# A chunked delta-rule attention with a feed-forward behind it: all work as tasks in an own order, with another mapping on TensorE

## The chip, the core and the metric

The kernel runs on one core of one Trainium2 chip. The metric is the device time of one execution in microseconds (us). Names of engines: PE is TensorE (PEld its weight loads), DVE is VectorE, ACT is ScalarE, POOL is GpSimd, SP is SyncE, which issues the transfers. L615 is line 615 of the kernel before; behind the change the line numbers are those of the new file.

## What is computed

Four batches of eight heads (32 in all), 768 steps, head size 40. Each head carries a 40 x 40 state; the rows of all heads then pass a layer norm and a feed-forward layer 320 -> 1280 -> 320.

```python
for t in range(S):
    kt, vt, rt = (k[:, :, t], v[:, :, t], r[:, :, t])
    wt, at, bt = (w[:, :, t], a[:, :, t], b[:, :, t])
    y[:, :, t] = np.einsum('bhd,bhde->bhe', rt, state)
    Sa = np.einsum('bhde,bhe->bhd', state, at)
    state_decay = state * wt[:, :, None, :] - np.einsum('bhd,bhe->bhde', Sa, bt)
    state = state_decay + np.einsum('bhd,bhe->bhde', vt, kt)
...
xn = (x - mu) / np.sqrt(var + 1e-06) * g_ln
ch = np.maximum(xn @ w_ch1, 0.0) @ w_ch2
return (x + ch).astype(np.float32)
```

## The kernel before

**Chunks.** The 768 steps are cut into 24 chunks of 32. Within a chunk the recurrence is turned into matrix products and one unit-triangular 32 x 32 system per head; from chunk to chunk only the state is carried. The 32 heads lie in two halves of 16, one at partitions 0 to 39 (or 0 to 31), one at 64 to 103.

**Preparation** (`prep`, L140 to L195): `wa` (decays and a) and `bk` (b and k) are loaded with the channel on partitions. Two scans (`gE` L149, `qE` L153) give the running products of the decays from both ends, `aT` (L160) and `bk` (L165) are scaled by them, on DVE for the first six chunks and on POOL behind them. ACT copies `aT` into a block-diagonal tile `abd` (L164), so that one matmul with 104 rows serves both halves (L178). The signed triangle `gk` (L183) goes to DRAM (`d_g`).

**Token rows** (`load_cl`, L309 to L345): the same decays, keys and b are loaded a second time with the token on partitions (`clt`), checked for values outside the range that the chunk form allows (`wild`, L315), scanned again (`gC` L321, `qC` L325), transposed on DVE (L329, L331) and multiplied on POOL into `xk` in eight small pieces a chunk (L339).

**Triangles.** Chunks are gathered into slabs of two or four, so that one system stands on each partition (64 or 128 of them). `invert2` (the first three slabs) inverts both 16 x 16 diagonal halves in 14 steps of two DVE instructions (L241, L245), and `solve2` joins them by three rounds of matmuls; `invert` (the other five slabs) inverts the whole 32 x 32 in 30 steps (L208, L211). The result goes to DRAM and comes back as `tt`.

**Chain** (`chain`, L366 to L393): the right-hand side (`prh`, L372), times the inverse (L357 in `solve`, L268 in `solve2`), copied into `x2` (L362, L279), the new state (L384), scaled into the next chunk's `x2` (L390). **Rows out** (`state` L401, `post` L416 to L447): transposes, the masked product with r (L429, L435), the output rows (L443), `xt` (L447). **Feed-forward** (`norm` L557 to L589, `moe` L593 to L637), called MoE in the code: two chunks make a group of 256 rows; for each of ten slices of 128 hidden units, eight matmuls (L615), a relu and its remainder (L618, L619), and six matmuls of the slice before (L601). Weights are converted from 64-bit floats at the start (L488 to L531).

**Order.** DVE and ACT run the first stage in the written order; behind it priorities (`BOOST`, `NUDGE`) and a scheduler's timeline decide. 180 matmuls on a constant (`warm`, L221) fill PE in the first 200 us. All transfers are issued by SP in one queue.

```python
def invert(si):
    ...
    for j in range(1, C - 1):
        ...
        nc.vector.tensor_tensor(
            out=tv, in0=y[0:n, j + 1:, j:j + 1].broadcast_to([n, m, j]),
            in1=y[0:n, j:j + 1, 0:j].broadcast_to([n, m, j]), op=ALU.mult)
        final["inv", si] = nc.vector.tensor_tensor(
            out=y[0:n, j + 1:, 0:j], in0=y[0:n, j + 1:, 0:j], in1=tv, op=ALU.add)
...
for q in range(4):
    hf, p = q % 2, 8 * (q // 2) + h
    nc.tensor.matmul(
        prh[32 * q:32 * q + 32, h], lhsT=X2s[RROW[hf], hf, 32 * p:32 * p + 32],
        rhs=X2[RROW[hf], hf, p, 0:D], start=True, stop=True)
```

## Time and profile before

| | before |
|---|---|
| median of 3 runs | 703.12 us (701.27 to 704.05) |
| the profiled execution | 704.42 us |
| its span, first to last instruction | 702.6 us |
| mean granted TensorE clock | 0.898 |
| moved by DMA | 92.35 MB, 158156 packets |

A row of a view of lines reads: line, engine, operation, output<-inputs, shapes and count, then busy time and the mean of one in ns, then the idle time of the engine just before these instructions and what ended most of it. A row of the timeline reads: start in us, length in us, engine, line, operation. A matmul in fp32 leaves two records, one in fp32r or a transpose one. Matmuls are pipelined, so two rows may overlap; what a batch costs is seen from the start of one to the start of the next.

### The profile page before, as it was taken

To read this page: it belongs to the slowest core of one execution; us is meant where nothing else is said; L and a number is where in the kernel's file an instruction comes from. 1 tells how busy PE (TensorE), PEld (TensorE's weight loads), DVE (VectorE), ACT (ScalarE), POOL (GpSimd) and SP (SyncE) were. 2 spreads that over 40 slices of the span, in tenths; PEclk is the share of its full clock that TensorE was granted. 3 is DMA by queue.
4 is the path that set the end of the run, shared out by engine and by line. 5 is a ranking of instruction groups with operands and counts; after the bars stand their busy time and mean duration, and the time that the engine had idled before them with its cause. 6 is when DMAs were issued, how large, how long until landed. Compare 5 with 4: busy or idle time off the path is not lost.

```text
span 702.6 us, 24730 instructions
## 1 busy us (share of the span) xinstructions
PE 579.0 (82%) x10386; PEld 511.0 (73%) x10386; DVE 564.0 (80%) x1291; ACT 328.7 (47%) x816; POOL 291.4 (41%) x328
## 2 busy tenths in 40 slices
PE   2787778786697879788878889798987899999994
PEld 2686666675586758776757778697776777889994
DVE  8969899899589967899957999788996999764621
ACT  4314664544243445363366356444656255666220
POOL 8606486757514246146505533543133312233000
PEclk9979796868588799899989899999999899999998
DMA  6787977538635467455558653775336435420100
GB/s 176 202 230 206 280 188 182 136 86 198 137 104 144 99 154 161 124 159 134 131 145 177 141 134 94 169 167 122 89 95 116 117 86 119 109 51 16 38 20 22
DMA packets 158156, 92.35 MB, mean 131 GB/s; under 512 B 126504, under 2 KB 136488, under 8 KB 158040
## 3 DMA queue, kind: packets, MB, share of 16 engines
q1 hardware_dynamic: 158040, 90.72, 52.2%
q8 instruction: 83, 1.36, 0.8%
q14 instruction: 33, 0.27, 0.1%
HBM read 72.06 MB, written 18.64 MB: 129 GB/s over the span
## 4 chain that ended last, share of the span: by engine, by line
DVE 45%; PE 26%; DMA 17%; issue 5%; ACT 3%; SPq 2%; POOL 1%; DVEq 0%; POOLq 0%; ACTq 0%
PE ps L615 8%; PE ps L601 7%; DVE yinv L211 6%; DVE ytmp L208 6%; DMA yinv<-d_g 6%; DMA wa<-in_et_dram 4%; DVE x L390 3%; DVE x5s L435 3%; DVE gE L149 3%; DVE qE L153 3%; DVE hl L619 2%; DMA tt<-d_tt 2%; DVE yinv L245 2%; DMA d_tt<-yinv 2%; DVE gC L321 2%
## 5 line engine op out<-in xcount | busy, mean ns | idle before, releaser
L615 PE MATMUL ps<-xh,w 128*128 128x256 f32 x480 | 117.4, 303 | 3.3 <-DVE xl L589 2.3
L601 PE MATMUL ps<-w,hh 128*128 128x320 f32 x480 | 113.4, 330 | 4.9 <-DVE yinv L211 3.6
L618 ACT ACTIVATE hh<-ps 128x256 fp32r<-128x256 f32 x120 | 45.6, 383 | 140.0 <-PE ps L615 130.9
L615 PEld LDWEIGHTS ps<-xh,w 128*128 128x128 f32 x480 | 87.2, 200 | 8.4 <-DVE xl L589 2.6
L601 PEld LDWEIGHTS ps<-w,hh 128*128 128x128 f32 x480 | 79.2, 197 | 8.9 <-ACT hh L618 5.7
L601 PE MATMUL ps<-w,hl 128*128 128x320 f32 x240 | 75.0, 335 | 12.5 <-DVE hl L619 11.9
L619 DVE SCALAR_TENSOR_TENSOR hl<-ps,hh 128x256 fp32r<-128x256 f32 x120 | 49.5, 414 | 43.2 <-ACT hh L618 40.7
L208 DVE TENSOR_TENSOR ytmp<-yinv 128x30 f32<-128x30 f32 (+19 forms) x150 | 61.7, 412 | 26.4 <-DMA yinv<-d_g 24.4
L165 POOL TENSOR_TENSOR bk<-bk,gE 104x1024 f32<-104x1024 f32 x18 | 41.9, 2327 | 91.7 <-DMA bk<-in_et_dram 71.2
L221 PE MATMUL ps<-start,ident 128*128 128x160 f32 x360 | 74.3, 363 | 0.0
L615 PE MATMUL ps<-xl,w 128*128 128x256 f32 x240 | 71.0, 296 | 0.0
L221 PEld LDWEIGHTS ps<-start,ident 128*128 128x128 f32 x360 | 63.4, 232 | 2.3
L211 DVE TENSOR_TENSOR yinv<-yinv,ytmp 128x30 f32<-128x30 f32 (+19 forms) x150 | 61.1, 408 | 2.3
L601 PEld LDWEIGHTS ps<-w,hl 128*128 128x128 f32 x240 | 45.7, 199 | 16.5 <-DVE hl L619 14.9
L615 PEld LDWEIGHTS ps<-xl,w 128*128 128x128 f32 x240 | 48.2, 201 | 0.5
L362 ACT COPY x<-ps_c 32x160 f32<-32x160 f32 x144 | 40.7, 283 | 12.9 <-PE ps_c L357 9.7
L160 POOL TENSOR_TENSOR aT<-wa,qE 104x512 f32<-104x512 f32 x18 | 25.6, 1423 | 50.8 <-DVE qE L153 41.0
L390 DVE TENSOR_TENSOR x<-ps_c,x2s 40x320 f32<-40x320 f32 x92 | 44.7, 486 | 2.1
L384 PE MATMUL ps_c<-x,xk 128*40 128x40 f32 (+1 forms) x1472 | 43.1, 213 | 3.9 <-ACT x L279 2.9
L164 ACT COPY abd<-aT 40x512 f32<-40x512 f32 x48 | 29.6, 616 | 35.4 <-DVE aT L160 19.6
L372 PE MATMUL ps_c<-x,x2s 96*32 96x40 f32 (+1 forms) x1536 | 30.5, 223 | 18.7 <-issue 6.6
L384 PEld LDWEIGHTS ps_c<-x,xk 128*40 128x40 f32 (+1 forms) x1472 | 37.0, 126 | 9.2 <-ACT x L279 3.5
(174 smaller groups left out, 1359.7 us busy)
## 6 DMA issues: line engine op xcount, KB each, us to landing
clt<-in_cl_dram SPq DMA_DIRECT2D x24, 485.5 KB
wa<-in_et_dram SPq DMA_DIRECT2D x20, 422.9 KB
bk<-in_et_dram SPq DMA_DIRECT2D x20, 416.0 KB
d_g<-gk SPq DMA_DIRECT2D x48, 128.0 KB
x<-in_vt_dram SPq DMA_DIRECT2D x48, 128.0 KB
d_a<-aT SPq DMA_DIRECT2D x24, 214.5 KB
vu<-in_vr_dram SPq DMA_DIRECT2D x24, 208.0 KB
x2s<-d_a SPq DMA_DIRECT2D x48, 82.5 KB
```

What stands on the lines that cost most here:

```text
L165: (nc.gpsimd if c >= EARLY else nc.vector).tensor_tensor(out=kb, in0=kb, in1=g[R, :, 0:C].unsqueeze(2).broadcast_to([104, 16, 2, C]), op=A ...
L208: nc.vector.tensor_tensor(out=tv, in0=y[0:n, j + 1:, j:j + 1].broadcast_to([n, m, j]), in1=y[0:n, j:j + 1, 0:j].broadcast_to([n, m, j]), o ...
L211: final["inv", si] = nc.vector.tensor_tensor(out=y[0:n, j + 1:, 0:j], in0=y[0:n, j + 1:, 0:j], in1=tv, op=ALU.add)
L221: nc.tensor.matmul(pw[:, 0:w], lhsT=ident, rhs=start0.rearrange("p h t -> p (h t)")[:, 0:w], start=True, stop=True)
L362: nc.scalar.copy(out=dst[:, :, :, j, 0:D], in_=pu[32 * j:32 * j + 32, :, :, hf])
L372: nc.tensor.matmul(prh[32 * q:32 * q + 32, h], lhsT=X2s[RROW[hf], hf, 32 * p:32 * p + 32], rhs=X2[RROW[hf], hf, p, 0:D], start=True, stop= ...
L384: nc.tensor.matmul(pst[r0:r0 + D, h], lhsT=XK[FROW[hf], 1, hf, p], rhs=X2[FROW[hf], hf, p, 0:D], start=True, stop=True)
L390: nc.vector.tensor_tensor(out=X2n[r0:r0 + D, hf, ps, 0:D], in0=pst[r0:r0 + D], in1=pc.unsqueeze(2).broadcast_to([D, 8, D]), op=ALU.mult)
L601: nc.tensor.matmul(po[u], lhsT=l[:, us], rhs=ws[f"w2_{f}"][:, x], start=f == 0 and n == 0, stop=f == 9 and n == 2)
L615: nc.tensor.matmul(ph, lhsT=l, rhs=r, start=n == 0, stop=n == 7)
L618: nc.scalar.activation(out=hh, in_=ph, func=AF.Relu)
L619: nc.vector.scalar_tensor_tensor(out=hl, in0=ph, scalar=0.0, in1=hh.bitcast(F32), op0=ALU.max, op1=ALU.subtract)
```

## The change

A new kernel for the same inputs and outputs. No engine is left to the scheduler any more. Every piece of work is a task with an engine, an assumed duration, a key, and the names that it reads and writes; `Plan.order` plays the tasks through once while the kernel is built and writes the instructions down in that order. PSUM is eight banks, four for the small batches (A), two for the first feed-forward layer and the norm (H), two for the second layer (M).

```diff
+class Plan:
+    HOP = 0.15
+    def add(self, eng, us, fn, key, rd=(), wr=(), opens=(), late=0.0, kb=0.0, room=()):
...
+    def order(self, free):
...
+            if t["eng"] == "SP" and len(dma) >= 8:
+                s = max(s, dma[-8])
...
+                s0 = min(ss)[0]
+                s, n = min(((s, n) for s, n in ss if s <= s0 + 0.05), key=lambda x: T[x[1]]["key"])
...
+    with tc.manual_schedule():
+        for t in P.order(dict(A=[0, 1, 2, 3], H=[4, 5], M=[6, 7])):
+            t["fn"]()
```

**Token rows by TensorE.** The second load, its scans, transposes and small POOL products (`load_cl`) are gone. `prep` turns the scaled `bk` and the products `q` by matmuls with the identity into `kt` (L355, L360, copied by ACT at L364). A transfer and an ACT copy (L437) bring them into `xk`. The check of the decays reads them again in their first layout (`wilds`), 24 loads of 80 x 528 through the two `wa` buffers.

```diff
-        nc.vector.tensor_tensor_scan(
-            out=flat(g), data0=t[:, 0:330], data1=flat(start0[:, 0:10]), initial=0.0,
-            op0=ALU.mult, op1=ALU.max)
...
-        nc.vector.transpose(out=gt.rearrange("p (g j) -> p j g", j=10), in_=g[:, :, 0:C])
...
+                    if x < 2:
+                        for hf, rs in enumerate(ROWS):
+                            p = 8 * x + h
+                            mm(px[ZROW[hf]:ZROW[hf] + 64, h], lhsT=tb[rs, 64 * p:64 * p + 64],
+                               rhs=ident[rs, rs], start=True, stop=True)
+                    else:
+                        for y in range(4):
+                            rs = ROWS[y // 2]
+                            mm(px[32 * y:32 * y + 32, h], lhsT=q[rs, 8 * (y % 2) + h, 1:33],
+                               rhs=ident[rs, rs], start=True, stop=True)
```

**Triangles by halves.** All slabs hold two chunks (12 slabs, 64 partitions). `invert` loads three 16 x 16 quarters (`yv`), inverts the two diagonal ones in 14 steps (L387, L391); `merge` builds the missing quarter and the transposed inverse `tt` by two batches of 32-row quadrants (L411, L421).

```diff
+        dma(k0, 64, DL, [("y", i, 0)], yr(2), d_l[s][0:B, :, 0:B].rearrange("a m t -> m a t"))
...
+        for j in range(1, B - 1):
...
+            for h in range(8):
+                for qs in QUADS:
+                    mm(po[qs, h], lhsT=hv[i][qs, h, 0:2 * B], rhs=hv[i][qs, h, 2 * B:3 * B], start=True, stop=True)
...
+                    mm(po[qs, h], lhsT=qm[i][qs, h], rhs=hv[i][qs, h, 3 * B:5 * B], start=True, stop=True)
```

**Quadrants instead of block diagonals.** `abd`, `rbd` and `hbd` are gone. The triangle (L328) and the masked product (L532) use 40-row operands at partitions 0 and 64 in turn, the solution and its transpose (L463, L503) 32-row quadrants; the state is transposed by a matmul with the identity (L519). Evictions of L532 are two of 64 x 512 (L537) instead of four of 64 x 256.

```diff
-                nc.tensor.matmul(
-                    pz[64 * bb:64 * bb + 64, :, h], lhsT=vu[R, p].rearrange("p x t -> p (x t)"),
-                    rhs=rbd[R, p], start=True, stop=True)
...
+            for p in range(16):
+                for hf, rs in enumerate(ROWS):
+                    mm(pz[ZROW[hf]:ZROW[hf] + 64, p], lhsT=vu[i][rs, p].rearrange("p x t -> p (x t)"),
+                       rhs=x5s[i][rs, hf, p], start=True, stop=True)
...
+                    mm(bank[bs[bb].at][UROW[hf]:UROW[hf] + C, h * D:h * D + D], lhsT=tt[i][qs, h], rhs=hn[i][qs, h],
+                       start=True, stop=True)
```

The feed-forward's matmuls are the same (L714, L698), `warm` is gone, the output tile `ot` has two buffers instead of one, and the fourth chunk (not the sixth) is the last that scales on DVE (`EARLY`).

**Where it moves on the engines.** On PE, in the middle of the program, one chunk's small batches before (L429 and L178 the products with block diagonals, L384 the state):

```order
L601 MATMUL ps_4413<-w_5_2423,hl 128x320
L586 MATMUL ps_4888<-ident,xn 128x128 x2
L429 MATMUL ps_a<-rbd,vu 64x2x32 x2
L178 MATMUL ps_a<-abd,bk_93 64x2x32 x16
L429 MATMUL ps_a<-rbd,vu 64x2x32 x14
L586 MATMUL ps_4888<-ident,xn 128x128
L384 MATMUL ps_c<-x_1_96,xk_102 40x40 x32
```

And now at such a place (L421 the join of the triangles, L355 and L360 the token rows, L482 the state, L698 the feed-forward between them):

```order
L421 MATMUL bank_144<-hv_88,qm_90 32x32 x32
L355 MATMUL bank_145<-ident,bk_75 64x40 x16
L698 MATMUL bank_148<-w_8_1987,hh_135 128x320 x2
L698 MATMUL bank_148<-w_8_1987,hl_137 128x320
L698 MATMUL bank_149<-w_8_1987,hh_135 128x320 x2
L698 MATMUL bank_149<-w_8_1987,hl_138 128x320
L360 MATMUL bank_142<-ident,qE_79 32x40 x32
L482 MATMUL bank_143<-x_0_93,xk_99 40x40 x16
```

Sixteen matmuls over 104 rows became 32 over 40 rows, and four kinds of batches came in that PE did not have. On DVE, an inversion before, where the steps of one 32 x 32 system stand between other work (L390 the state, L149 to L153 the scans of a later chunk, L315 and L321 token rows):

```order
L208 TENSOR_TENSOR ytmp<-yinv 128x30
L390 TENSOR_TENSOR x_0_95<-ps_c,x2s_97 40x8x40 x2
L211 TENSOR_TENSOR yinv<-yinv,ytmp 128x30
L390 TENSOR_TENSOR x_0_95<-ps_c,x2s_97 40x8x40 x2
L208 TENSOR_TENSOR ytmp<-yinv 128x58
L149 SCALAR_TENSOR_TENSOR gE<-wa_91,start_88 104x528
L315 SCALAR_TENSOR_TENSOR wild<-clt,wild 128x320
L321 SCALAR_TENSOR_TENSOR gC<-clt,start_88 128x330
L211 TENSOR_TENSOR yinv<-yinv,ytmp 128x29x2
```

And now, slab 1 (`yv_85`), from the fill that waits for the slab's three loads:

```order
L379 MEMSET yv_85 64x16 x2
L387 TENSOR_TENSOR ytmp_86<-yv_85 64x28
L391 TENSOR_TENSOR yv_85<-yv_85,ytmp_86 64x2x14
L387 TENSOR_TENSOR ytmp_86<-yv_85 64x52
L391 TENSOR_TENSOR yv_85<-yv_85,ytmp_86 64x2x13x2
L387 TENSOR_TENSOR ytmp_86<-yv_85 64x72
L391 TENSOR_TENSOR yv_85<-yv_85,ytmp_86 64x2x12x3
```

The steps stand in a longer run behind the loads, with little between. On SP, the first transfers before and now (`wa`, `bk` the first chunks' inputs; `gt`, `rx`, `r_` weights; `vu` rows of v):

```order
L135 DMA wa_91<-in_et_dram 40x1041
L137 DMA wa_91<-in_et_dram 24x1041
L135 DMA wa_91<-in_et_dram 40x1041
L135 DMA bk_93<-in_et_dram 40x1024
L137 DMA bk_93<-in_et_dram 24x1024
L135 DMA bk_93<-in_et_dram 40x1024
```

```order
L227 DMA gt<-in_gl_dram 128x3
L227 DMA rx<-in_w1x_dram 128x640
L227 DMA r_0_0_223<-in_w_dram 128x256
L227 DMA r_1_0_224<-in_w_dram 128x256
L227 DMA r_0_225<-in_w_dram 128x320
L227 DMA r_1_226<-in_w_dram 128x320
L227 DMA vu_101<-in_vr_dram 40x16x32 x2
L227 DMA wa_73<-in_ea_dram 40x1041 x2
```

The first chunk's inputs now stand behind eight other transfers.

More of the change, by code (lines that the diff above doesn't have):

```diff
@@ L22 @@
 C = 32
+B = C // 2
 D = 40
@@ L474, in words @@
+    ws, raw, W1X = {}, {}, []
+    def weights():
+        dma(-2.0, 2, (), ["gt"], gt, gl)
+        op("ACT", 0.25, -1.8, (), ["gt"], lambda: nc.scalar.mul(out=gt, in_=gt, mul=2.0 ** -8))
+        raw["x"] = const.tile([128, FF], F32, name="rx", tag="w1x")
+        dma(-1.5, 655, (), [("w", "x")], raw["x"].bitcast(U64), w1x_in)
         def words(i):
@@ L762, in moes @@
-    def moes():
-        for g in range(NCH // 2):
-            while normed[0] < 2 * g + 2:
-                if normed[0] in xts:
-                    norm(normed[0])
-                    normed[0] += 1
-                yield
-            yield from moe(g, [out[2 * g], out[2 * g + 1]], g + 1 < NCH // 2)
-    def preps(first):
-        for c in range(first, NCH):
-            for i, _ in enumerate(p[c]):
-                if i < 2 and c + 2 < NCH:
-                    load_e(c + 2, [i])
-                yield
@@ L855, in body @@
     nc.vector.memset(ones, 1.0)
-    pf = ps_c.tile([1, 1], F32, name="ps_c")
-    nc.tensor.matmul(pf, lhsT=any_w, rhs=ones, start=True, stop=True)
+    fbank = [pf_.tile([128, 512], F32, name=f"fb{i}") for i in range(5)]
+    pf = fbank[0][0:1, 0:1]
+    mm(pf, lhsT=any_w, rhs=ones, start=True, stop=True)
     flag = const.tile([1, 1], mybir.dt.int32, name="flag")
```

1284 lines of the change are left out of this document (586 added, 698 removed).

## The prediction

> **What bounds the kernel now.** I read the totals first, then the same span in stretches.
>
> ```profile
> span 702.6 us, 24730 instructions
> PE 579.0 (82%) x10386; PEld 511.0 (73%) x10386; DVE 564.0 (80%) x1291; ACT 328.7 (47%) x816; POOL 291.4 (41%) x328
> DVE 45%; PE 26%; DMA 17%; issue 5%; ACT 3%; SPq 2%; POOL 1%; DVEq 0%; POOLq 0%; ACTq 0%
> ```
>
> The first row is the span, the second the busy time of each engine, the third the chain of waits that ended last. No engine is full: VectorE leads the chain, TensorE is as busy. The stretches show how the two share the time (their columns: length, PE, PEld, DVE, ACT, POOL busy, then granted TensorE clock, DMA share, GB/s).
>
> ```profile
> 0.00:35.00 35.00, 17.87 (x160) 16.75 (x160) 31.36 (x46) 14.10 (x18) 27.20 (x43) 0.98 0.70 189
> 50.00:100.00 50.00, 37.66 (x796) 32.91 (x794) 45.52 (x90) 25.29 (x59) 30.22 (x27) 0.86 0.85 232
> 100.00:150.00 50.00, 36.95 (x745) 31.42 (x747) 45.71 (x92) 25.67 (x63) 30.88 (x32) 0.76 0.60 149
> 250.00:350.00 100.00, 83.88 (x1564) 72.78 (x1563) 85.16 (x196) 48.49 (x126) 46.14 (x48) 0.91 0.60 148
> 350.00:450.00 100.00, 83.83 (x1516) 73.08 (x1515) 83.90 (x203) 49.79 (x131) 39.62 (x42) 0.91 0.59 139
> 450.00:550.00 100.00, 87.87 (x1617) 76.03 (x1617) 81.05 (x212) 55.67 (x145) 33.97 (x48) 0.95 0.53 125
> 550.00:650.00 100.00, 94.75 (x1770) 83.06 (x1768) 76.67 (x197) 56.04 (x148) 31.47 (x45) 1.00 0.34 78
> ```
>
> Two readings. In each 100 us from 250 to 650, PE and DVE busy add up to 168 to 171 us: when one has more to do the other gets less done, because chunk work and feed-forward work (MoE in the code) hand over between them. I call this sum **1.69** and use it as the coupling of two engines that work in fixed orders. And PE reached 0.95 once DVE needed only 0.77. Up to 150 us DVE is the full one (31.36 of 35, 45.5 of 50), and the feed-forward begins late:
>
> ```profile
> L615 PE MATMUL ps<-xh,w x480: 276/281/582, 136.0 to 691.5; 128*128 128x256 f32 x160
> ```
>
> **The change, engine by engine.** Everything is reissued, so I sum work, not edits.
>
> *TensorE.* Its price is the time from the start of one batch to the start of the next.
>
> ```profile
> 676.39 1.88 PE ps L615 x16
> 678.27 0.88 PE ps L601 x6
> 634.84 0.28 PE L615 MATMUL ps<-xl,w1x 128*128 128x256 f32 x1
> 635.05 0.80 PE L372 MATMUL ps_c<-x,x2s 96*32 96x40 f32 x64
> 635.78 0.83 PE L401 MATMUL ps_a<-ident,x 40*104 40x40 f32 x16
> 636.55 0.56 PE L601 MATMUL ps<-w,hh 128*128 128x320 f32 x2
> 636.94 0.31 PE L601 MATMUL ps<-w,hl 128*128 128x320 f32 x1
> 313.33 1.43 PE L384 MATMUL ps_c<-x,xk 128*40 128x40 f32 x64
> 314.68 0.38 PE L615 MATMUL ps<-xh,w 128*128 128x256 f32 x1
> 95.13 0.79 PE L268 MATMUL ps_c<-hbd,tt 32*32 32x40 f32 x64 [0.30 <-DVE hbd L275]
> ```
>
> Feed-forward, unchanged: 8 first-layer matmuls 0.94, six second-layer 0.88, times 120 = 218 us. Small fp32 batches are 64 records for 32 matmuls. With four 32-wide column groups at work and 40 moving columns a batch takes 0.73 (L372); with two 64-wide groups 1.35 (L384). The new shapes per chunk, by the nearest of these: L360, L452, L463, L547 four groups, 0.75 each, 3.0; L421 and L503 the same with 32 columns, 0.6 each, 1.2; L411 with 16 columns, 0.5; the pairs L355, L482, L519 two groups, 1.35 each, 4.05; L328 and L532 two groups with 32 columns, 1.1 each, 2.2. That is 10.95 a chunk, 263 in all (the old batches, priced so, were 7.5). L463 and L503 could run at the two-group rate (+1.1 a chunk), and the 32- and 16-column ones could gain nothing from being short (+0.9): bounds 10.95 to 13; below, nothing faster than 0.5 a batch is shown, so 9.5. Norm transposes about 7. Each stay in tile shapes costs about 0.1 going in (634.84 to 635.05 instead of 0.12) and 0.1 coming out (two matmuls in 0.39 instead of 0.29); the new order has 138 such stays, 28 us. Sum **516 us** at full clock, against about 445 before plus the 360 warming records (L221), which go.
>
> The Trainium skill (TensorEngine Tiling, Key Properties) says that changing the tiling mode, not only the tile, drains TensorE. The trace agrees for tile to full array, about 0.1 each way, but not for L372 to L401, whose 64 records start 0.73 apart with no gap. If all 612 batch borders of the new order drained, it would be 61 us instead of 28 and the time would come out near 657.
>
> *VectorE.*
>
> ```profile
> L149 DVE TENSOR_TENSOR_SCAN gE<-wa,start 104x528 f32<-104x528 f32 x24 | 32.5, 1352 | 7.3 <-POOL bk L165 3.6 <-DMA wa<-in_et_dram 3.6
> L208 DVE TENSOR_TENSOR ytmp<-yinv 128x30 f32<-128x30 f32 (+19 forms) x150 | 61.7, 412 | 26.4 <-DMA yinv<-d_g 24.4
> L211 DVE TENSOR_TENSOR yinv<-yinv,ytmp 128x30 f32<-128x30 f32 (+19 forms) x150 | 61.1, 408 | 2.3
> L241 DVE TENSOR_TENSOR ytmp<-yinv 64x28 f32<-64x28 f32 (+6 forms) x42 | 18.1, 430 | 2.7 <-issue 2.0
> L241 DVE TENSOR_TENSOR ytmp<-yinv x42: 155/260/2092, 34.4 to 169.1; 64x28 f32<-64x28 f32 x6, 64x52 f32<-64x52 f32 x6, 64x72 f32<-64x72 f32 x6, 64x88 f32<-64x88 f32 x6
> 34.45 0.15 DVE L241 TENSOR_TENSOR ytmp<-yinv 64x28 f32<-64x28 f32 x1 [0.65 <-issue]
> 41.52 0.18 DVE L241 TENSOR_TENSOR ytmp<-yinv 64x28 f32<-64x28 f32 x1
> 193.74 1.17 POOL L160 TENSOR_TENSOR aT<-wa,qE 104x512 f32<-104x512 f32 x1 [6.43 <-DVE qE L153]
> 193.84 1.20 DVE L208 TENSOR_TENSOR ytmp<-yinv 128x108 f32<-128x108 f32 x1
> L165 POOL TENSOR_TENSOR bk<-bk,gE 104x1024 f32<-104x1024 f32 x18 | 41.9, 2327 | 91.7 <-DMA bk<-in_et_dram 71.2 <-DVE yinv L211 9.2 <-PE ps_a L401 7.7
> L496 DVE TENSOR_SCALAR m<-m 128x320 uint32<-128x320 uint32 (+1 forms) x22 | 12.1, 556 | 0.0
> L183 DVE TENSOR_TENSOR gk<-ps_a,sign 128x512 f32<-128x512 f32 x19 | 12.8, 673 | 0.9 <-PE ps_a L178 0.9
> L325 DVE TENSOR_TENSOR_SCAN qC<-clt,last 128x330 f32<-128x330 f32 x24 | 20.2, 842 | 0.2
> ```
>
> The inversion does not become small: 192 step pairs become 168 (14 in each of 12 slabs), on fewer elements. An undisturbed slab ran its 28 instructions from 34.45 to 41.7, 0.26 us each; the mean of the same line is 0.43, with single ones up to 2.1. Between 0.26 and 0.43 I take 0.33, because the long ones stand beside POOL's (193.84: 1.20 us while POOL's multiply ran, where its like took 0.27), and POOL's work falls from 291 to about 120 us: L160 and L165 stay with 20 calls each, 75 us, the 192 small multiplies of L339 go. So 110 us (bounds 87 to 145) instead of 158. The second set of scans, transposes and checks per chunk (L315 to L331, about 96 us) goes; a wider check of the decays comes back, 24 at about 0.75, 18 us. The masked copy becomes 48 of 512 elements at 0.67, 32 instead of 40. The rest keeps count and form. Sum **481 us** instead of 564.
>
> *ScalarE* gains transposed-key copies and loses others: about 335 us, half the time, not a bound. *DMA* moves some 74 MB instead of 92 and fewer small packets.
>
> *SyncE* issues 742 transfers instead of about 510. A plain one takes it 0.33 to 0.37, so 270 us; no bound, but at the start it counts.
>
> ```profile
> 2.04 0.33 SPq L135 DMA_DIRECT2D bk<-in_et_dram  x1
> 6.47 1.26 DVE L149 TENSOR_TENSOR_SCAN gE<-wa,start 104x528 f32<-104x528 f32 x1 [0.47 <-DMA wa<-in_et_dram]
> GB/s 176 202 230 206 280 188 182 136 86 198 137 104 144 99 154 161 124 159 134 131 145 177 141 134 94 169 167 122 89 95 116 117 86 119 109 51 16 38 20 22
> ```
>
> Now 1.95 MB of weights and rows (640 + 2 x 256 + 2 x 320 + 2 x 80 KB) are issued ahead of the first chunk; at 280 GB/s, the most a slice shows, that is 7 us, so the first scan starts near 10.5 instead of 6.5.
>
> **The sum.** The feed-forward can start when both chunks of the first pair are normed. In VectorE's new order 97 us of work stand from the first scan to the second `xl` (7 chunks' first scans, 29 step pairs, all 22 weight conversions at about 1.3, L496 and the two lines behind it). VectorE was busy 0.88 of the first 150 us, so 97 becomes 110 and the feed-forward starts near **120 us** instead of 136 to 152. Behind that stand, on TensorE, 516 less 46 (the batches ahead of the first feed-forward matmul in its order) = 470, at a granted clock of 0.98 (0.95 to 1.00 in the late stretches) 479; on DVE 481 less 97 and 4 of fills = 380. 859 / 1.69 = **508 us**, in which PE is busy 0.94, just what it has reached. The end:
>
> ```profile
> 692.00 1.62 PE ps L601 x11
> 694.16 2.98 DMA out_dram<-ot
> 697.27 0.49 DVE ot L634
> ```
>
> The last matmul ended 9 us before the end, 3 of it because the second `ot` waited for the first one's transfer; with two buffers about 7, the check of the decays included. 120 + 508 + 7 = 635. The profiled run took 704.4 for a span of 702.6, and the median is 1.3 below it: **636 us**.
>
> **Rivals.**
>
> *The quadrants do not overlap (slower).* L328, L355, L519 and L532 alternate 40-row operands at partitions 0 and 64 into one bank. If such a pair runs one after the other, each batch doubles: +4.9 a chunk, some 98 us for the 20 chunks behind the start, TensorE's 479 becomes 579, and alone at 0.95 that is 610: 737 us. It decides from +3.3 us a chunk. Against it stands L268, four 32-row quadrants into one bank, 64 records in 0.79, as fast as four column groups with full rows. For it: no row shows a 40-row pair that alternates. The Trainium skill (TensorEngine Tiling, Gotcha 1: PSUM Pressure) says different row tiles cannot use the same PSUM bank at once; L268 does not bear that out, so I leave this at 0.12.
>
> *The wait for the triangle takes the place of its work.* The new order puts a slab's 28 steps behind three loads of 64-byte pieces, with nothing else of VectorE between. Before, five such loads cost 24.4 us of DVE idle (the L208 row), 4.9 each; twelve would cost 59: 695 us, and 670 to 720 with what follows on the other engines. For it: SyncE's extra issues make each load later. Against it: slabs of two chunks are prepared two chunks ahead. 0.19, of which 0.09 ends faster, 0.04 within 0.5%, 0.06 slower.
>
> *VectorE is freed more than I count.* Steps at 0.26 and a sum of 1.75 as POOL falls silent: (479 + 355) / 1.75 = 477, 604 us. 0.09.
>
> **How the numbers follow.** Forecast 0.60 (about 605 to 690, the bounds of the small batches and of the steps), quadrants 0.12, late triangles 0.19, freed VectorE 0.09. The predicted time is the forecast's. The range takes in the freed VectorE and most of the late triangles: 595 to 708. Within 0.5%, about what a measurement of this kernel can tell from no change: faster 0.60 + 0.09 + 0.09 = 0.78, same 0.04, slower 0.12 + 0.06 = 0.18.
>
> **What would show it.** Right: the first feed-forward matmul near 120 us; DVE near 480 us busy and the step lines near 0.33 us; from 200 us on PE busy above 0.9 and PE and DVE together near 1.69; batches of L355 and L519 near 0.7 for 32 records. Wrong: 32 records of L355 taking 1.3 us (quadrants in turn), VectorE idle before L379 or L387 by several us a slab with a transfer named (late triangles), a low granted clock after 200 us, or ScalarE and DVE both idle while SyncE waits.

## The result and the profile after

| | before | after |
|---|---|---|
| median of 4 runs | 703.59 us (701.27 to 706.89) | 778.87 us (767.59 to 783.47) |
| ratio, 95% interval | | 1.0958 (1.0841 to 1.1076), slower |
| the profiled execution, its span | 704.42, 702.6 us | 774.97, 773.3 us |
| mean granted TensorE clock | 0.898 | 0.904 |
| TensorE's records | 10386 | 20122 |
| VectorE, GpSimd busy | 564.0, 291.4 us | 440.1, 113.9 us |
| moved by DMA | 92.35 MB | 77.60 MB |

Runs over 1.5% above the fastest of their kernel count as slow and are left out of all times below; of the changed kernel two are left, 771.3 us in the mean. By the ratio the kernel became 67 us slower; 636 us, 67 us faster, was forecast. First the page of the changed kernel: span, busy time of each engine, and the chain of waits that ended last.

```profile
span 773.3 us, 43979 instructions
PE 688.8 (89%) x20122; PEld 642.2 (83%) x20122; DVE 440.1 (57%) x1078; ACT 324.3 (42%) x815; POOL 113.9 (15%) x106
PE 84%; issue 7%; DVE 3%; DMA 2%; SPq 1%; ACT 1%; POOL 1%; DVEq 0%; POOLq 0%
```

VectorE led the chain with 45% before; now it has 3% and TensorE has 84%. TensorE is the bound, and the work that left VectorE and GpSimd bought nothing here. The same stretches as before (length; PE, PEld, DVE, ACT, POOL busy; granted clock; DMA share; GB/s):

```profile
50.00:100.00 50.00, 29.18 (x926) 27.59 (x922) 43.03 (x97) 22.92 (x56) 21.32 (x18) 1.00 0.50 129
100.00:150.00 50.00, 44.57 (x1360) 41.31 (x1356) 25.58 (x54) 24.01 (x61) 14.68 (x14) 0.90 0.47 116
250.00:350.00 100.00, 95.33 (x2888) 88.20 (x2888) 55.47 (x147) 41.72 (x104) 13.39 (x8) 0.88 0.39 97
350.00:450.00 100.00, 95.81 (x2940) 89.39 (x2937) 57.58 (x149) 38.18 (x96) 13.32 (x8) 0.88 0.41 99
450.00:550.00 100.00, 95.32 (x3103) 88.11 (x3105) 59.54 (x155) 42.59 (x110) 10.04 (x6) 0.95 0.40 95
550.00:650.00 100.00, 93.60 (x2723) 87.12 (x2716) 50.72 (x127) 36.63 (x94) 9.95 (x6) 0.86 0.40 99
```

From 250 us on PE is busy 0.94 to 0.96, as forecast for its best stretches, but PE and DVE add up to only 144 to 155, and the clock is 0.86 to 0.95. The feed-forward begins late (times of the first and last record):

```profile
L714 PE MATMUL bank<-xh,w x480: 277/281/582, 149.4 to 763.8; 128*128 128x256 f32 x160
```

What a batch costs is seen in the timeline, from the start of one to the start of the next:

```profile
297.74 2.06 PE L328 MATMUL bank<-aT,bk 40*64 40x32 f32 x64
299.73 0.56 PE L698 MATMUL bank<-w,hh 128*128 128x320 f32 x2
...
300.80 1.13 PE L355 MATMUL bank<-ident,bk 40*64 40x40 f32 x32
301.86 0.80 PE L452 MATMUL bank<-x,x2s 96*32 96x40 f32 x64
302.59 0.73 PE L411 MATMUL bank<-hv 32*32 32x16 f32 x64
```

L328 takes 1.99 us, 31 ns a record; a half of L355 takes 1.06, 33 ns a record; L452, with 32 columns of weights, 0.73 or 11.4 ns a record. Further on in the same window stands what the busy shares hide:

```profile
304.52 0.28 PE L714 MATMUL bank<-xh,w1x 128*128 128x256 f32 x1 [0.30 <-issue]
304.64 0.28 PE L714 MATMUL bank<-xl,w1x 128*128 128x256 f32 x1
304.76 0.49 PE L681 MATMUL bank<-ident,xn 128*128 128x128 f32 x3
305.18 0.74 PE L463 MATMUL bank<-hn,tt 32*32 32x40 f32 x59
305.74 0.21 PE L421 MATMUL bank<-hv,qm 32*32 32x32 f32 x1
305.74 0.21 PE L463 MATMUL bank<-hn,tt 32*32 32x40 f32 x4
305.77 0.21 PE L421 MATMUL bank<-hv,qm 32*32 32x32 f32 x1
305.77 0.20 PE L463 MATMUL bank<-hn,tt 32*32 32x40 f32 x1
305.78 0.81 PE L421 MATMUL bank<-hv,qm 32*32 32x32 f32 x57
308.26 0.25 PE L421 MATMUL bank<-hv,qm 32*32 32x32 f32 x5 [1.67 <-issue]
```

TensorE stops in the middle of a batch for 1.67 us, and nothing that the profile shows releases it. From the first pause to the second it ran 1 + 1 + 3 + 59 + 1 + 4 + 1 + 1 + 57 = 128 records. The pauses stand such distances apart elsewhere too: between 150 and 700 us the trace has 24 of over 0.5 us, and the numbers of records between them are multiples of 128, less at most four (some records are missing in a trace). The page's list of DMA queues names the other side: transfers on a queue called "instruction" (packets, MB, share of 16 engines), before in the first row, after in the row of the next fence, and after between 250 and 450 us in the last.

```profile
q8 instruction: 83, 1.36, 0.8%
```

```profile
q8 instruction: 159, 2.61, 1.4%
...
q8 instruction: 46, 0.75, 1.6%
```

One packet is 16.4 KB, and 46 packets go with the 5828 records of these 200 us: 127 records each. The whole programs give the same, 125 records a packet before and 127 after: TensorE's own instructions arrive in blocks of 128 records. The pauses fit these arrivals: each of the 24 ended 1.0 to 1.7 us after a packet had landed, and packets come some 4 us apart. At a resolution of an eighth of a us, no two of the 46 came closer than 3.4 us, and distances of 3.4 to 3.9 us are found also where few data moved (425.1 to 428.6, with the DMA engines 0.15 busy). A block of 11 ns records is used up in 1.5 us, one of 31 ns records in 4. The pauses show up in the view of TensorE's waits under `issue` (us in total, times, longest); its largest and its smallest row:

```profile
PE bank L421 <- issue: 11.4, 10, 2.4
...
PE bank L452 <- issue: 0.2, 1, 0.2
```

All such rows of the changed kernel add up to 37.1 us, those of the kernel before to 7.3.

### The profile page after: what moved, and what is told of

The parts are those of the page before. It is cut to its first block, busy times and chain, and to the rows that moved or that the text cites. A ratio compares the mean times of both kernels' runs of the same rounds, so it can differ in the third digit from the quotient of the medians.

```text
span 773.3 us, 43979 instructions
## 1 busy us (share of the span) xinstructions
PE 688.8 (89%) x20122; PEld 642.2 (83%) x20122; DVE 440.1 (57%) x1078; ACT 324.3 (42%) x815; POOL 113.9 (15%) x106
## 2 busy tenths in 40 slices
DMA packets 130656, 77.60 MB, mean 100 GB/s; under 512 B 102432, under 2 KB 108576, under 8 KB 130464
## 4 chain that ended last, share of the span: by engine, by line
PE 84%; issue 7%; DVE 3%; DMA 2%; SPq 1%; ACT 1%; POOL 1%; DVEq 0%; POOLq 0%
PE bank L698 17%; PE bank L714 17%; PE bank L532 7%; PE bank L355 7%; PE bank L328 7%; PE bank L482 5%; PE bank L519 5%; PE bank L360 3%; PE bank L547 3%; PE bank L452 3%; PE bank L503 2%; PE bank L463 2%; PE bank L421 2%; PE bank L411 2%; PE bank L681 1%
## 5 line engine op out<-in xcount | busy, mean ns | idle before, releaser
L698 PE MATMUL bank<-w,hh 128*128 128x320 f32 x480 | 127.5, 353 | 1.4 <-ACT tt L423 1.4
L714 PE MATMUL bank<-xh,w 128*128 128x256 f32 x480 | 119.0, 309 | 0.0
L355 PE MATMUL bank<-ident,bk 40*64 40x40 f32 x1536 | 76.8, 273 | 22.0 <-POOL bk L317 14.3
L714 PEld LDWEIGHTS bank<-xh,w 128*128 128x128 f32 x480 | 90.2, 207 | 1.8
L355 PEld LDWEIGHTS bank<-ident,bk 40*64 40x64 f32 x1536 | 70.7, 186 | 24.9 <-POOL bk L317 14.4
L698 PEld LDWEIGHTS bank<-w,hh 128*128 128x128 f32 x480 | 84.1, 207 | 6.1 <-issue 1.6
L698 PE MATMUL bank<-w,hl 128*128 128x320 f32 x240 | 79.2, 330 | 0.0
L714 PE MATMUL bank<-xl,w 128*128 128x256 f32 x240 | 71.7, 299 | 0.2 <-DVE xl L686 0.2
L364 ACT COPY kt<-bank 128x320 f32<-128x320 f32 x72 | 30.6, 425 | 75.9 <-PE bank L355 48.8
L328 PE MATMUL bank<-aT,bk 40*64 40x32 f32 x1536 | 61.2, 241 | 0.1
L328 PEld LDWEIGHTS bank<-aT,bk 40*64 40x64 f32 x1536 | 58.5, 161 | 1.8 <-issue 0.2
L532 PEld LDWEIGHTS bank<-x5s,vu 40*64 40x64 f32 x1536 | 53.9, 151 | 4.0 <-ACT xk L522 0.9
L519 PE MATMUL bank<-ident,x 40*40 40x40 f32 x1536 | 45.5, 221 | 13.1 <-POOL x L280 8.8
L532 PE MATMUL bank<-x5s,vu 40*64 40x32 f32 x1536 | 56.7, 233 | 0.0
L519 PEld LDWEIGHTS bank<-ident,x 40*40 40x40 f32 x1536 | 39.2, 133 | 16.4 <-POOL x L280 8.8
L391 DVE TENSOR_TENSOR yv<-yv,ytmp 64x28 f32<-64x28 f32 (+6 forms) x168 | 49.1, 293 | 5.8
L387 DVE TENSOR_TENSOR ytmp<-yv 64x28 f32<-64x28 f32 (+6 forms) x168 | 48.5, 289 | 5.5
```

What stands on the lines that cost most here:

```text
L328: mm(pg[64 * hf:64 * hf + 64, p], lhsT=tb[rs, 64 * p:64 * p + 64], rhs=at[rs, 32 * p:32 * p + 32], start=True, stop=True)
L355: mm(px[ZROW[hf]:ZROW[hf] + 64, h], lhsT=tb[rs, 64 * p:64 * p + 64], rhs=ident[rs, rs], start=True, stop=True)
L387: nc.vector.tensor_tensor(out=tv, in0=yb[:, :, j + 1:, j:j + 1].broadcast_to(S), in1=yb[:, :, j:j + 1, 0:j].broadcast_to(S), op=ALU.mult)
L391: nc.vector.tensor_tensor(out=v, in0=v, in1=tv, op=ALU.add)
L519: mm(pt[rs, h], lhsT=x2[i][rs, hf, 8 * bb + h], rhs=ident[rs, rs], start=True, stop=True)
L532: mm(pz[ZROW[hf]:ZROW[hf] + 64, p], lhsT=vu[i][rs, p].rearrange("p x t -> p (x t)"), rhs=x5s[i][rs, hf, p], start=True, stop=True)
```

## The experiments

Three theories. **Price**: the 40-row pairs cost more of the array than forecast. **Supply**: the stream of instructions holds TensorE up, by the number of records. **Clock**: the order of small batches and feed-forward lets the granted clock fall. "Waits" below is the sum of all `issue` rows of TensorE; records, waits and clock are those of the profiled execution. The runs are from several chips, on which the kernel before took 702.7 to 708.0 us, so differences of a few us are not read.

| run | what differs from the changed kernel | us | records | waits, us | clock |
|---|---|---|---|---|---|
| after | | 771.3 | 20122 | 37 | 0.904 |
| e1 | two banks for L532; halves of L328 one after the other | 844.8 | 20122 | 33 | 0.878 |
| e2 | 64-column weights cut in two | 846.3 | 24730 | 142 | 0.877 |
| e3 | feed-forward spread between the small batches | 793.5 | 20122 | 44 | 0.902 |
| e4 | L355 as one-record transposes | 748.0 | 18970 | 38 | 0.929 |
| e5 | L328, L532 on four tiles | 757.3 | 20122 | 49 | 0.912 |
| e6 | e4 and e5 | 737.9 | 18970 | 43 | 0.897 |
| e7 | e6, and L519 on four tiles | 740.6 | 18970 | 63 | 0.901 |
| e8 | e6, few records | 673.2 | 14938 | 5 | 0.931 |
| e9 | e6, few records, wide | 671.2 | 14746 | 5 | 0.927 |
| e10 | few records alone | 712.1 | 16090 | 5 | 0.929 |
| e11 | e6, whole triangles from chunk 9 on | 717.2 | 17050 | 29 | 0.908 |
| e12 | e11 in another order | 682.0 | 17050 | 29 | 0.945 |

### Do two halves run beside each other? (e1, e5)

```diff
-            pz = bank[b.at].rearrange("p (n t) -> p n t", t=C)
             for p in range(16):
                 for hf, rs in enumerate(ROWS):
+                    pz = bank[bs[hf].at].rearrange("p (n t) -> p n t", t=C)
...
-            for p in range(16):
-                for hf, rs in enumerate(ROWS):
+            for hf, rs in enumerate(ROWS):
+                for p in range(16):
                     mm(pg[
```

> The changed kernel with two edits to the order and place of 40-row matmuls, nothing left out: L532 writes its two halves into two PSUM banks instead of one, still in turn; L328 issues the 16 matmuls of the first half and then the 16 of the second, instead of in turn. In the changed kernel a full batch of either takes 1.98 us from its start to the start of the next batch (64 records, 31 ns each). Theory A, the halves could run beside each other but meet in one bank: the L532 batch falls to about 1.0 to 1.2 us, 24 of them give 20 us, time near 757 us, and L328 stays at 1.98 or gets longer. Theory B, the price of a record follows the width of its weights and the halves never run beside each other: both stay at 1.98 us within 0.05, time 770 to 785 us.

In e1's timeline:

```profile
360.79 3.71 PE L328 MATMUL bank<-aT,bk 40*64 40x32 f32 x64
364.43 0.72 PE L698 MATMUL bank<-w,hh 128*128 128x320 f32 x2
...
381.04 2.06 PE L532 MATMUL bank<-x5s,vu 40*64 40x32 f32 x64
383.03 0.56 PE L698 MATMUL bank<-w,hh 128*128 128x320 f32 x2
```

Neither theory stands. The bank makes no difference: L532 stays at 1.99. But L328 needs 3.64 us when one half follows the other, 57 ns a record, against 31 in turn. So the halves do run beside each other; what was wrong is what one of them costs. A tile of 40 rows and 64 columns is held 57 to 62 ns by a record, and two tiles in turn halve that. The Trainium skill (TensorEngine Tiling (Array Packing), Gotcha 1: PSUM Pressure) says that different row tiles cannot use the same PSUM bank at once; this run does not bear that out as a price (1.99 us with one bank and with two). The whole of e1 became 74 us slower for some 40 us of array work (24 x 1.65); the time at half clock rose with it, from 148 to 205 us.

If a tile is held and other tiles are free, four in turn must halve it again. In e5 odd heads write to the other half of the output rows, so the two row halves meet both column halves:

```diff
-                    mm(pz[ZROW[hf]:ZROW[hf] + 64, p], lhsT=vu[i][rs, p].rearrange("p x t -> p (x t)"),
+                    pz, r0 = bank[bs[hf].at].rearrange("p (n t) -> p n t", t=C), ZROW[hf ^ p % 2]
+                    mm(pz[r0:r0 + 64, p], lhsT=vu[i][rs, p].rearrange("p x t -> p (x t)"),
                        rhs=x5s[i][rs, hf, p], start=True, stop=True)
```

> The changed kernel with L328 and L532 writing heads with an odd number to the other half of the output rows, each half of the weights' rows to a bank of its own, so that four tiles (two by rows, two by columns) take turns instead of two; VectorE reads the product in four pieces instead of one or two; nothing left out. e1 showed 59 ns a record with one tile in a row and 31 with two in turn. Theory E, a tile is held 59 to 62 ns by a record and different tiles run beside each other: four in turn give 15.5 ns a record, 1.0 us for the 64 records of either batch instead of 1.98, 47 us of TensorE's time less. Rival, two at once is the most there is for this shape: 1.98 stays, time 780 to 800. With E and no other bound the time falls by about 55 us to 725; with theory C (blocks of 128 records at 3.5 us or more, 157 of them as in the changed kernel) the waits for instructions rise from 37 to 60 us or more and the time stays above 740.

```profile
285.65 1.14 PE L537 MATMUL bank<-x5s,vu 40*64 40x32 f32 x64
286.72 0.56 PE L707 MATMUL bank<-w,hh 128*128 128x320 f32 x2
```

1.07 us, 16.7 ns a record (L537 is L532 moved down by the edit): the theory holds, and that is the price that the prediction had put down (1.1). The array's work fell by 44 us, the time by 14. The waits rose from 37 to 49 us, less than expected.

### The one-record transposes (e4), and both together (e6)

```diff
-                        for hf, rs in enumerate(ROWS):
-                            p = 8 * x + h
-                            mm(px[ZROW[hf]:ZROW[hf] + 64, h], lhsT=tb[rs, 64 * p:64 * p + 64],
-                               rhs=ident[rs, rs], start=True, stop=True)
+                        rs = ROWS[x]
+                        nc.tensor.transpose(out=px[:, h], in_=tb[rs, 128 * h:128 * h + 128], identity=ident[rs, rs])
```

> The changed kernel with the key transposes of L355 done as 16 one-record transposes of 40 rows by 128 columns (one half per bank, two heads each) instead of 32 two-record matmuls with 64-column weights, and four ScalarE copies of 64 partitions instead of two of 128; nothing left out. Theory B and a TensorE-bound kernel: 16 records at some 57 ns (47.5 ns at 104 columns in the kernel before) are 0.9 us a chunk instead of 2.12, 29 us less, time near 750 us. Theory C: 2304 records fewer are 18 blocks fewer, which alone are worth up to 18 x 3.6 = 65 us, so the time falls by more than the array's 29 us where the blocks are the bound. Rival, VectorE or the DMAs set the time and TensorE only looks busy: within 10 us of 779.

748.0 us, 23 less. Eight transposes take 0.61 us, 77 ns each and not 57, so the array saved 0.9 us a chunk, 22 us, about the time that was gained. The expectation had miscounted the records: 1152 go, 9 blocks, not 2304. The waits did not fall with them (38 for 37): the stream got shorter, but the array's work too.

> e5 and the one-record transposes of e4 together; nothing left out. If E holds, the small batches of a chunk cost 11.1 us at full clock, what the prediction put down (10.95) instead of the changed kernel's 14.0. If that price was the prediction's only error, the time is 625 to 650 us. Theory C and the clock (granted 0.90 to 0.93 and not 0.98, waits for instructions 40 to 60 us) give 120 + (493 - 50) / 0.95 + 50, some 25 us for the clock and the rest for waits: 690 to 715 us.

737.9 us. With its small batches at the prediction's price (11.1 us a chunk at full clock, 10.95 forecast) the kernel is still 102 us above the forecast. The price was not the only error, nor the larger one. TensorE was busy 71 us less than in the changed kernel (617.6 for 688.8), but only 37 us of it show in the profiled spans: its waits for other engines rose by 29 us and those for instructions by 6.

### Is it the stream of instructions? (e2, e7, e8, e9, e10)

e2 makes the batches shorter and the stream longer:

```diff
-                    mm(pz[ZROW[hf]:ZROW[hf] + 64, p], lhsT=vu[i][rs, p].rearrange("p x t -> p (x t)"),
-                       rhs=x5s[i][rs, hf, p], start=True, stop=True)
+                    rs, z0 = ROWS[hf], ZROW[hf] + C * x
+                    mm(pz[z0:z0 + C, p], lhsT=vu[i][rs, p, x], rhs=x5s[i][rs, hf, p], start=True, stop=True)
```

> The changed kernel with the 64-column weights of L328, L355 and L532 cut into two matmuls of 32 columns each, nothing left out. The changed kernel's trace shows 31 to 33 ns a record for 64 columns (1.98 us for 64 records), 23 for 40 columns, and 11.4 for 32 columns (L452, L547: 0.73 us for 64), whatever the rows. Theory B, width sets the price and TensorE's array is the bound: 128 records at 11.4 are 1.46 us for L328 and L532, L355 takes 0.73 instead of 1.06 twice a chunk, together 1.7 us a chunk, 41 us, time near 738 us. Theory C, TensorE's instructions come in blocks of 128 records at no less than 3.5 us each and this stream is as tight as the array: 24730 records are 193 blocks instead of 157, 193 x 3.6 = 695 us of them behind a start that needs few, so the batches get shorter as B says but the time that TensorE waits for its own instructions rises from 37 us to over 100, and the time is 780 to 840 us.

Its page (busy time, queue, chain) and one batch of its timeline (L535 is L532):

```profile
PE 661.3 (78%) x24730; PEld 602.3 (71%) x24730; DVE 439.7 (52%) x1078; ACT 324.7 (39%) x815; POOL 114.7 (14%) x106
q8 instruction: 195, 3.19, 1.6%
PE 74%; issue 16%; DVE 4%; ACT 2%; SPq 2%; DMA 1%; POOL 0%; DVEq 0%; POOLq 0%; ACTq 0%
```

```profile
308.51 1.29 PE L535 MATMUL bank<-x5s,vu 40*32 40x32 f32 x128
309.73 0.56 PE L700 MATMUL bank<-w,hh 128*128 128x320 f32 x2
```

The batch shrank from 1.99 to 1.22 us, the array has some 50 us less to do (an estimate, 24 times the three batches' gain), and the kernel is 75 us slower: 36 more blocks brought 105 us more of waits. The tasks and their order are the changed kernel's, so that is the supply; the rest is the lower clock, which stood at half for 206 us instead of 148.

e7 gives the counter-test, less array work with the same records (the diff is e5's, on L519):

> e6 and, besides, the state transposes of L519 with four tiles in turn (odd heads to the other rows, a bank for each half of the rows); nothing left out. Theory E: 46 ns a record in one tile gives 11.6 ns with four in turn, 0.74 us a chunk instead of 1.48, 18 us of TensorE's time in all. If the array alone set the time, it falls from e6's 738 us to about 715; theory C (the blocks of instructions, whose number does not change) says that most of it comes back as waits: 728 to 738 us, waits for instructions above e6's 43 us.

L519's 64 records took 0.66 to 0.76 us instead of 1.48. 18 us of array work went, the time did not move (740.6 against 737.9), and the waits rose from 43 to 63.

e8 turns it round: the same array time, fewer records. e9 does the same with matmuls that fill the array, and e10 takes e8's edit to the changed kernel without e6's.

```diff
-                        for y in range(4):
-                            rs = ROWS[y // 2]
-                            mm(px[32 * y:32 * y + 32, h], lhsT=q[rs, 8 * (y % 2) + h, 1:33],
-                               rhs=ident[rs, rs], start=True, stop=True)
+                        nc.tensor.transpose(out=px[:, h], in_=ident[0:D, 0:128], identity=ident[0:D, 0:D])
```

In e9 there stands in the place of L360, twice a batch:

```diff
+                        mm(bank[b.at][:, 160 * h:160 * h + 160], lhsT=ident,
+                           rhs=start0.rearrange("p h t -> p (h t)")[:, 0:160], start=True, stop=True)
```

> e6 with L360, L411 and L421 replaced by 8 one-record transposes of the identity matrix each (so the decay matrices, the joined triangles and all that follows from them are not computed): 24 records a chunk instead of 192, at some 0.6 us each for 0.66 to 0.73, so TensorE's array time falls by 0.2 us a chunk, 5 us in all, while 4032 records or 31 blocks of instructions go. Theory C: the waits for instructions fall from 43 to under 15 us, the time from 738 to 670 to 700 us. Rival, array time and clock set the time: 725 to 738 us.

> As e8, with matmuls of the whole identity matrix (128 columns of weights, 128 or 160 moving columns, two or three a batch, 0.5 to 0.75 us) in the place of the transposes: as few records, and the same time of the array within 10 us, but the array full in it. Theory D2, the granted clock follows how full the array has been over the last 3.4 us, and waits pull it down: the clock rises from e8's to 0.95 or more and the time is 15 to 35 us below e8's. Rival, only waits of TensorE pull the clock down: e8 and e9 have the same clock within 0.015 and the same time within 8 us.

> The changed kernel (two tiles in turn, L355 as it was) with the replacement of e8: 8 one-record transposes of the identity in the place of L360, L411 and L421, so the decay matrices, the joined triangles and what follows from them are not computed. With the changed kernel (779 us), e6 (738) and e8 (673) this fills a table of two by two: dear or cheap pairs, many or few records. If the two causes add up, 779 - 65 = 714 us, and the waits for instructions fall from 37 to under 8 us. If the dear pairs give the stream of instructions time to catch up, few records are worth less here than with cheap pairs: 730 to 755 us.

e8's page:

```profile
PE 584.6 (87%) x14938; PEld 536.9 (80%) x14938; DVE 464.1 (69%) x1198; ACT 345.2 (51%) x863; POOL 117.2 (17%) x106
q8 instruction: 118, 1.93, 1.2%
PE 74%; DVE 8%; DMA 6%; ACT 5%; SPq 3%; issue 3%; DVEq 0%
```

The replaced batches took 0.60 to 0.61 us each in e8 and mostly 0.6 to 0.8 in e9, close to what they took before, and both kernels lost 65 us or more, 2 us for each of the 32 blocks that went. The four kernels make a table:

| us | all records | 4032 records fewer |
|---|---|---|
| pairs as in the changed kernel | 771.3 (after) | 712.1 (e10) |
| cheap pairs | 737.9 (e6) | 673.2 (e8) |

The price is worth 33 and 39 us, the records 59 and 65. Within the spread of the runs the causes add up, and the larger is the one that the prediction didn't have. In the profiled executions the records' worth is half waits and half busy time: from e6 to e8 the waits for instructions fell by 38 us and TensorE's busy time by 33. With the pauses gone TensorE is full: in e10 it was busy 0.99 to 1.00 of each 100 us from 250 to 650. One reserve: the replacements no longer wait for the tiles that the originals read. Those waits are 7.6 us in the changed kernel (`qE` 5.8, `qm` 1.8) and 15 in e6, but TensorE's waits for other engines and transfers did not fall as a whole: 41 us in the changed kernel and 40 in e10, 70 in e6 and 75 in e8.

### What pulls the clock down? (e3, e9)

In the changed kernel every run of small batches of over 7 us shows a fall of the clock to half: in six of the ten 3.3 to 4.9 us into it, in the others 7 to 9. e3 breaks the runs up:

```diff
+                def ff(n):
+                    if e != "PE":
+                        return False
+                    return T[n]["slice"] != group // 20 + 1 if small >= 1.3 else T[n]["slice"] > 0 or T[n]["us"] == 0.4
-                s, n = min(((s, n) for s, n in ss if s <= s0 + 0.05), key=lambda x: T[x[1]]["key"])
+                s, n = min(((s, n) for s, n in ss if s <= s0 + 0.05), key=lambda x: (ff(x[1]), T[x[1]]["key"]))
```

> The changed kernel with one rule added to the plan's order and nothing else: after 1.3 us (planned) of small batches TensorE takes a feed-forward slice if one of the current pair is ready, and until then it prefers small batches. Theory D, the granted clock falls to half some 4 us into a run of small batches that no feed-forward slice interrupts (in the changed kernel each run of over 7 us shows it, 140 of the 650 us from 100 to 750 at half): the long runs after the start go, the mean clock rises from 0.90 to 0.95 or more, the half-clock time falls to under 50 us, and the time falls by 30 to 45 us to 735 to 750. Rival, the clock falls for another reason (idle time of TensorE, waits for instructions): the clock stays within 0.02 of 0.90 and the time within 12 us of 779. Theory C adds that the demand for instructions becomes even, so the 37 us of waits for instructions fall to under 20.

The theory falls: behind 150 us no run of small batches was longer than 7.3 us, yet the clock stayed at 0.902, the waits rose to 44 us, and the kernel was no faster. Of its 13 falls to half between 200 and 650 us, 11 had 0.6 us or more of waiting in the 4 us ahead. e9 takes the other variant away: with as few records as e8 but the array full in the replaced batches, clock and time were e8's. Nor do the waits set it. From e6 to e8 it rose from 0.897 to 0.931, but a second run of e6 had 0.922 and a second run of e8 0.908, e4 has 38 us of waits and 0.929, and the kernel before has 7 us and 0.898. What sets the clock stays open.

### A version that beats both (e11, e12)

If records are what is dear, work that TensorE got for its many small matmuls should go back. L411 and L421 are 128 records a chunk; the kernel before had inverted whole triangles on VectorE, which now has room.

```diff
+FIRST = (0, 2, 4, 6, 9, 12, 15, 18, 21)
+SLABS = [range(x, y) for x, y in zip(FIRST, FIRST[1:] + (NCH,))]
+TWO = 4
...
+        if s >= TWO:
+            y = y[0:n].rearrange("p a t -> p (a t)").rearrange("p (a t) -> p a t", t=C)
...
+            for j in range(1, C - 1):
...
+                op("DVE", 0.8, k0 + 0.01 * j, (), two("y", i, 3) + [("ot", 2)], f)
```

> e6 with the triangles from chunk 9 on inverted whole on VectorE, three chunks at a time, as the kernel before does, so that L411 and L421 are left to the first nine chunks; nothing of the computation left out. 15 x 128 = 1920 records or 15 blocks and 20 us of the array's time go; VectorE gets 5 x 24.6 us (the 60 steps of the kernel before at 0.41 us) for 5 x 1.5 x 8.1 us of halves, about 60 us more, 525 us in all. Theory C: 738 - 20 - 15 x 2 = 685 to 700 us, below both kernels. Rival, VectorE's long inversions are late and TensorE waits for the triangles: 705 to 750 us.

717.2 us, ratio 1.0148 (1.0069 to 1.0226) to the kernel before: the time lies in the rival's range. The waits for instructions fell to 29 us, but TensorE waited 59 us for VectorE instead of 18, which I put down to the inversions' key: it put them ahead of everything else.

```diff
-        k0 = c0 - 2.0 if len(SLABS[s]) == 2 else c0 - 2.7
+        k0 = c0 - 2.0
...
-                op("DVE", 0.8, k0 + 0.01 * j, (), two("y", i, 3) + [("ot", 2)], f)
+                op("DVE", 0.8, k0 + 0.02 * j, (), two("y", i, 3) + [("ot", 2)], f)
```

> e11 with other numbers in its plan and nothing left out: the batches on TensorE that were planned at 0.45 to 0.8 us stand at about their measured length, the three chunks of a slab are prepared 0.4 chunks earlier, and the 60 steps of a whole inversion come 0.7 chunks later and with a key that rises twice as fast, so that VectorE does its other work between them. In e11 TensorE waited some 50 us for VectorE (decays 23, second layer's operand 15, first layer's 12). If those waits came from inversions done in one piece, they fall under 20 us and the time from 717 to 680 to 700 us, below both kernels. If VectorE (523 us busy) and the stream of instructions (135 blocks) hold it up in any order: 705 to 720 us.

e12's page:

```profile
span 680.7 us, 38084 instructions
PE 572.6 (84%) x17050; PEld 525.1 (77%) x17050; DVE 517.1 (76%) x1263; ACT 331.0 (49%) x813; POOL 115.6 (17%) x104
q8 instruction: 135, 2.21, 1.4%
PE 66%; DVE 14%; issue 8%; ACT 4%; DMA 3%; SPq 2%; POOL 1%; DVEq 0%; POOLq 0%; ACTq 0%
```

682.0 us, ratio 0.9657 (0.9605 to 0.9709): faster than both kernels, with the whole computation in it. TensorE's waits for VectorE fell from 59 to 35 us (not under 20), and the clock rose to 0.945. Since lengths, preparation and keys changed together, the gain isn't divided among them.

## Why the prediction was wrong

**The missing term: records.** The prediction counted TensorE's work in array time alone. It noted the `issue` 5% of the chain and went past it, and gave no price to 9736 more records. That is the failed step with the largest worth: 59 to 65 us by the table, for 4032 records; with these gone the waits are down to 5 us.

**The price of the pairs.** The step "the pairs L355, L482, L519 two groups, 1.35 each, 4.05; L328 and L532 two groups with 32 columns, 1.1 each" was wrong: measured were 1.98 for L328 and for L532, 2.12 for L355 and 1.48 for L482 and L519. The short ones were low too (L421 0.68, L503 0.74 for 0.6; L411 0.66 for 0.5); those at 0.75 were right. Together 14.0 us a chunk for 10.95, above the upper bound of 13. The reasoning, that four 32-row quadrants were as fast as four column groups and so two 40-row halves would be as fast as two groups, counted tiles in turn, rightly; it took the price from 40-column weights (L384) and let a batch with fewer moving columns be cheaper. It is the weights' columns that set it: 57 to 62 ns a tile at 64, 46 at 40 (2 x 23), 46 at 32 (4 x 11.4). L355 took 1.06 us for its 32 records, between the 0.7 named as a sign of being right and the 1.3 named for quadrants in turn. The kernel before had the right row all along:

```profile
523.24 1.15 PE L429 MATMUL ps_a<-rbd,vu 104*64 104x64 f32 x32
524.22 0.88 PE L384 MATMUL ps_c<-x,xk 128*40 128x40 f32 x12
```

32 records with 64 columns of weights, two column groups in turn, 0.98 us: 31 ns each, with 64 moving columns as with L328's 32. The change kept that price and doubled the records. The rival that the quadrants don't overlap named the right lines and a price near it (+4.9 a chunk, deciding from +3.3, measured +3.1), but its mechanism fell in e1. The table gives this error 33 to 39 us. A drain at every border of two batches is not seen: L355, L452 and L411 start 1.06 and 0.73 us apart, and that is their price with the border in it.

**The clock.** 0.98 was taken from late stretches of the kernel before; 0.86 to 0.95 was granted. The trace has the clock at 1.00 or 0.50 and at nothing between, so 0.904 means some 19% of 773 us at half, 148 us. L452's batch takes 1.22 there instead of 0.73, so 148 us at half lose about 59 (an estimate), where 0.98 would lose 12. The time did not follow this rule alone: e6 took 737.98 us at 0.897 and 737.91 at 0.922, where the rule gives 15 us of difference. The kernel before, with 0.898 over its whole span, could have warned of it.

The three terms make 24 x 3.1 = 74, 37 of waits, and 47 of clock, 158 us, for a miss of 135. They overlap: the forecast's 508 us already held 29 in which TensorE stood still (508 less 479), and cheaper pairs came back in part as waits (e6). How the miss divides among the three is therefore not shown; what is shown are the differences in the table.

**The start.** The feed-forward began at 149.4 us, not near 120: 135.5 in e6 and 129.7 in e8, so 20 of the 29 us went with the two errors above; from 100 us on TensorE was already the full engine (44.57 of 50). The other 10 us are a start that was forecast too early: the first scan began at 12.5 us for 10.5, and where the other 8 lie is not shown. In e8, which has the forecast's price and few records, the remaining 37 us are these 10 and some 26 behind the start.

**The coupling.** The sum of PE and DVE busy, 1.69 in the forecast, fell to 1.44 to 1.55. It had been read where two engines hand work to and fro; it says nothing once one of them is the bound. The limit that stood beside it, PE at 0.95, held in the changed kernel only because of the pauses: with few records PE was busy 0.97 (e8) and 0.99 to 1.00 (e10).

**What was right, and what was luck.** VectorE's work did fall, to 440 us. The 481 put down does not follow from the prediction's own terms: 564 less 48 for the steps, 96 for the second scans and 8 for the masked copies, plus 18 for the check, is 430. With 430 the same division gives 606 us instead of 636, so this slip moved the forecast towards the result by 30 us. The steps took less than the 0.33 us put down, 98 us for 110.

```profile
L391 DVE TENSOR_TENSOR yv<-yv,ytmp 64x28 f32<-64x28 f32 (+6 forms) x168 | 49.1, 293 | 5.8
L387 DVE TENSOR_TENSOR ytmp<-yv 64x28 f32<-64x28 f32 (+6 forms) x168 | 48.5, 289 | 5.5
```

GpSimd (114 for 120), ScalarE (324 for 335) and the DMAs (77.6 MB for 74) came out near. The late triangles fell as a rival; VectorE's waits name them with 8.2 us in all, not 59:

```profile
DVE yv L379 <- DMA yv<-d_l: 8.2, 3, 3.8
```

Freed VectorE (604 us) asked for the wrong engine: VectorE was freed, and TensorE waited only 7.5 us for it.

## What to carry to other kernels

Where a change multiplies small matmuls, count instructions as well as array time: here a block of 128 records came no faster than every 3.4 us, and beyond that shorter batches only lengthened the pauses. Look for `issue` pauses in the middle of a batch at equal distances in records before trusting a busy share. And take the price of a tile from the same width of weights, with the same number of tiles in turn.

## What the runs showed of the hardware

- Records on different tiles run beside each other, on one tile they don't: 57 ns a record with one tile of 40 rows and 64 columns at work, 31 with two in turn, 16.7 with four (L328, L532 in e1, after, e5). Two PSUM banks instead of one changed nothing (1.99 us).
- TensorE's instructions arrive in packets of 16 KB for 128 records; 46 to 50 of them came in 200 us at most (after, e2), the closest 3.4 us apart.
- Stretches at half clock had lengths near multiples of 3.4 us (3.5, 6.75, 10.25, 13.75 in the changed kernel). The Trainium skill (TensorE: Matmul & The Clock Gate, What's actually happening) says that the gate looks at free-running windows of about 3.4 us; the trace agrees with that length.
- A transpose of 40 rows by 128 columns in one record took 77 ns, as much as nearly seven records with 32 columns of weights on four tiles (11.4).
